# One more pair of key tiles of one query group moved from ScalarE's exponential to VectorE's, with a new written-out order

## The chip, the cores and the metric

The kernel runs on one core of a Trainium2 chip. The metric is the device time of one execution in microseconds (us); lower is better. The engines are named as in the profile: PE is TensorE, ACT is ScalarE, DVE is VectorE, POOL is GpSimd, and SP is SyncE, which only issues DMAs.

## The reference

The input `x` has 2048 rows of 640 numbers. It is normalised, goes through an attention of 32 heads of width 20 (branch A) and through a gated two-stage MLP (branch B), and the two are multiplied and added to `x`:

```python
def _A_ref(x, wqkv, wo):
    ...
    scores = jnp.einsum("bhqd,bhkd->bhqk", q, k) * (Dh ** -0.5)
    p = _softmax(scores, axis=-1)
    o = jnp.einsum("bhqk,bhkd->bhqd", p, v)
    ...
x = A_x
xn = _layernorm(x, axis=-1)
s = _A_ref(xn, A_wqkv, A_wo)
g = _silu(_B_ref(xn, B_w1, B_w2, B_w3, B_w4))
return x + s * g
```

The exponentials of the softmax are 32 x 2048 x 2048 numbers, and they are most of the work outside TensorE.

## The kernel before

**Groups.** The heads go in eight quads of four heads, the queries in four groups of 512 (`qc`). One quad and one `qc` make a group of attention work; "group 3_3" is the last query group of quad 3, and "group 4_0" comes next. There are 32 groups, the last of which (7_3) has code of its own. In a group the 2048 keys are 16 key tiles of 128.

**A key tile on ScalarE.** TensorE makes the scores of the four heads (tasks `sc...`, each one head, 128 keys by 512 queries, one PSUM bank). ScalarE takes two heads at a time through one exponential of 128x1024 (`exp_act`, L1707) into SBUF. Where one wide PSUM tile is free, one instruction takes all four heads (128x2048, L1684). One `pv` task of four matmuls (L1447) multiplies with the values and adds into the one accumulation bank of the group.

**A block on both engines.** A "block" is a pair of key tiles (`BLK`: (2,3), (6,7), (10,11), (14,15), (0,1)). `score_both` makes, for each of the two tiles, the scores of all four heads; ScalarE takes two heads of each tile, and VectorE the other two. VectorE's way to an exponential has two steps. First it turns each score tile of 128x512 into a 16-bit integer with a scale and an offset (`u...` tasks, L1729), whose bits read as bf16 are a coarse power of two. Then three shifted copies of that integer tile are made by adding a constant (`s..._1` to `s..._3`), and the four versions are multiplied with the values and added up on TensorE (`pvd...` tasks, L1629: four versions for each block, four matmuls each). A shifted copy is one VectorE instruction (L1617, 128x4096 where two blocks share one, 128x2048 where a block is alone) or one GpSimd instruction (L1615). `PP` lists which go to GpSimd: shifts 2 and 3 of the unit that starts with block 0, and shift 3 of the one that starts with block 2. A block that stands alone as number 4 (`(6, 0, 1)` in `UNITS`) has its three shifts on VectorE.

**How many blocks.** `ND[quad][qc]` says how many blocks a group has. Most groups have four; eleven of the 32 have five (1_0, 2_0, 3_0, 4_0, 4_2, 5_0, 5_2, 6_0, 6_1, 6_2, 7_0). `order` takes the key tiles that are left over for ScalarE alone.

**Two ways to make scores.** A `sc` task is one matmul that uses 32 of TensorE's rows ("row form", L1638; the four heads of a tile then run side by side), or four matmuls over all rows and 32 columns each ("column form", L1655). All other work on TensorE is in column form. In `follow` a score task next to another one gets the row form, a lone one the column form.

**What fills TensorE.** The MLP of branch B, the projections of later heads (`mm_tile`, L748) and their evictions on VectorE (`gt`, `sev`, `vev`, `bo`) stand between the score and value matmuls. In group 3_3 ScalarE also does two of the four long GELUs (L2110).

**The order.** Nothing is scheduled at run time. `program` lists some 6,950 tasks with what they read and write; `TABLE` is one long string that names the tasks in the order in which they are emitted, and after each task the PSUM banks (seven for rotating tiles, one for the accumulation) and SBUF slots that it takes. `follow` reads it, and each engine executes its tasks in the order of the string, waiting on semaphores for what a task needs. Two characters are a task, and each further one a bank or a slot.

Of the kernel before, what the change touches and what calls it, by code (L numbers as in the profile page):

```python
# [671 lines left out]
class Gen:  # L672
# [1621 lines left out]
```

## Time and profile before

| | |
|---|---|
| median of three runs | 779.2 us (778.91 to 779.86) |
| the profiled execution | 780.64 us, of which 778.9 us lie between its first and its last instruction |
| granted TensorE clock, mean | 0.997 |
| busy: PE / ACT / DVE / POOL | 767.8 / 761.1 / 701.4 / 441.3 us |
| instructions | 28,219 |

A row of a group of instructions reads: line, engine, operation, tiles, count, then busy time, the mean duration of one, and the idle time of the engine just before them with what ended it. Durations of neighbouring instructions overlap (each engine is a pipeline), so the busy time of a group, which counts overlapped time once, divided by its count is nearer to what one instruction costs than the mean duration. Matmul ends are modelled, and four matmuls of column form run side by side.

### The profile page before, as it was taken

To read this page: it belongs to the slowest core of one execution; us is meant where nothing else is said; L and a number is where in the kernel's file an instruction comes from. 1 tells how busy PE (TensorE), PEld (TensorE's weight loads), DVE (VectorE), ACT (ScalarE), POOL (GpSimd) and SP (SyncE) were. 2 spreads that over 40 slices of the span, in tenths; PEclk is the share of its full clock that TensorE was granted. 3 is DMA by queue.
4 is the path that set the end of the run, shared out by engine and by line. 5 is a ranking of instruction groups with operands and counts; after the bars stand their busy time and mean duration, and the time that the engine had idled before them with its cause. 6 is when DMAs were issued, how large, how long until landed. Compare 5 with 4: busy or idle time off the path is not lost.

```text
span 778.9 us, 28219 instructions
## 1 busy us (share of the span) xinstructions
PE 767.8 (99%) x12594; PEld 296.5 (38%) x12594; DVE 701.4 (90%) x1177; ACT 761.1 (98%) x802; POOL 441.3 (57%) x238
## 2 busy tenths in 40 slices
PE   8999999999999999999999999999999999999996
PEld 4433333334444333233534334333334333333454
DVE  8889899988999999998988889999998899997786
ACT  7999999999999999999999999999999999999995
POOL 6386745564547657566464664766553635635742
PEclk9999999999999999999999999999999999999998
DMA  5315343364112423433343232324431023114443
GB/s 173 51 57 116 97 85 77 63 163 77 20 39 46 77 64 81 81 66 75 59 115 57 24 71 56 74 58 87 111 52 33 9 54 93 21 19 109 129 142 104
DMA packets 141353, 58.13 MB, mean 75 GB/s; under 512 B 113728, under 2 KB 136432, under 8 KB 141232
## 3 DMA queue, kind: packets, MB, share of 16 engines
q1 hardware_dynamic: 141232, 56.33, 32.8%
q8 instruction: 99, 1.62, 0.9%
q14 instruction: 22, 0.18, 0.1%
HBM read 34.70 MB, written 10.33 MB: 58 GB/s over the span
## 4 chain that ended last, share of the span: by engine, by line
PE 55%; ACT 41%; DVE 2%; DMA 1%; SPq 1%; issue 0%
ACT arena L1707 36%; PE psum L748 20%; PE psum L1638 14%; PE psum L1629 9%; PE psum L1447 7%; PE psum L1655 2%; ACT arena L2110 1%; ACT arena L1684 1%; ACT arena L2018 1%; DMA arena<-in_A_wqkv_dram 1%; SPq L935 1%; PE psum L1504 1%; ACT arena L2138 1%; PE psum L1478 1%; PE psum L1508 0%; DVE arena L1729 0%
## 5 line engine op out<-in xcount | busy, mean ns | idle before, releaser
L1707 ACT ACTIVATE arena<-psum 128x1024 bf16<-128x1024 f32 x730 | 675.0, 1075 | 5.8 <-PE psum L1638 3.7
L1615 POOL TENSOR_TENSOR arena<-arena 128x2048 int32<-128x2048 int32 x92 | 330.3, 3600 | 212.9 <-DVE arena L1617 126.3
L1729 DVE TENSOR_SCALAR arena<-psum 128x512 uint16<-128x512 f32 x532 | 342.8, 682 | 30.9 <-PE psum L1638 24.4
L748 PE MATMUL psum<-arena 128*32 128x320 bf16 (+1 forms) x5808 | 335.2, 333 | 0.4 <-ACT arena L1102 0.2
L1638 PE MATMUL psum<-arena 32*128 32x512 bf16 x1872 | 242.7, 384 | 1.4 <-ACT arena L1707 0.6
L1629 PE MATMUL psum<-arena 128*22 128x512 bf16 x2128 | 186.0, 382 | 0.2
L748 PEld LDWEIGHTS psum<-arena 128*32 128x32 bf16 x5808 | 138.2, 96 | 120.8 <-issue 44.2
L1638 PEld LDWEIGHTS psum<-arena 32*128 32x128 bf16 x1872 | 65.3, 91 | 208.9 <-ACT arena L1707 111.5
L1447 PE MATMUL psum<-arena 128*22 128x512 bf16 x1452 | 138.7, 382 | 0.0
L1617 DVE TENSOR_SCALAR arena<-arena 128x4096 uint16<-128x4096 uint16 (+1 forms) x124 | 133.7, 1095 | 1.0 <-PE psum L1629 0.2
L1629 PEld LDWEIGHTS psum<-arena 128*22 128x22 bf16 x2128 | 48.0, 90 | 63.4 <-issue 42.2
L1761 POOL TENSOR_TENSOR arena<-arena 128x512 bf16<-128x512 f32 x30 | 41.5, 1383 | 32.6 <-DVE arena L1617 27.6
L1447 PEld LDWEIGHTS psum<-arena 128*22 128x22 bf16 x1452 | 35.0, 90 | 52.0 <-issue 35.1
L1655 PE MATMUL psum<-arena 128*32 128x512 bf16 x476 | 46.3, 380 | 0.3
L2103 DVE CAST arena<-psum 128x512 bf16<-128x512 f32 x48 | 32.7, 684 | 3.8 <-PE psum L748 3.6
L1314 DVE CAST arena<-psum 128x512 bf16<-128x512 f32 x40 | 27.1, 685 | 4.7 <-PE psum L748 4.3
L1926 POOL TENSOR_TENSOR arena<-arena 128x640 bf16<-128x640 bf16 x12 | 16.8, 1402 | 21.5 <-DVE arena L1860 5.5
L959 DVE BATCH_NORM_STATS2 arena<-arena 128x6 f32<-128x320 bf16 x54 | 24.4, 477 | 1.6 <-DMA arena<-in_A_x_dram 1.6
L1748 DVE STREAM_TRANSPOSE arena<-psum 128x512 f32<-128x512 f32 x30 | 21.3, 711 | 2.5 <-PE psum L1629 1.5
L1860 DVE SCALAR_TENSOR_TENSOR arena<-psum,arena 128x320 bf16<-128x320 f32 x32 | 15.5, 486 | 8.3 <-PE psum L748 8.0
L1684 ACT ACTIVATE arena<-psum 128x2048 bf16<-128x2048 f32 x12 | 22.8, 1900 | 0.0
L2132 DVE TENSOR_TENSOR arena<-psum,arena 128x320 bf16<-128x320 f32 x32 | 15.6, 489 | 7.4 <-PE psum L748 7.2
(135 smaller groups left out, 340.9 us busy)
## 6 DMA issues: line engine op xcount, KB each, us to landing
arena<-in_B_w_dram SPq DMA_DIRECT2D x48, 160.0 KB, 2.7
arena<-arena SPq DMA_DIRECT2D x124, 32.0 KB, 1.9
arena<-in_B_w_dram SPq DMA_DIRECT2D x4, 960.0 KB, 5.5
arena<-in_A_x_dram SPq DMA_DIRECT2D x8, 320.0 KB, 5.5
arena<-in_A_x_dram SPq DMA_DIRECT2D x16, 160.0 KB, 3.0
out_dram<-arena SPq DMA_DIRECT2D x16, 160.0 KB, 2.6
heads<-arena SPq DMA_DIRECT2D x120, 20.0 KB, 2.0
arena<-keys SPq DMA_DIRECT2D x28, 80.0 KB
```

Of the source, the lines that this page charges most:

```text
L748: ins = e.matmul(pb[32 * c:32 * c + 32, 0:N], lhsT(k, c), rhs(k, c), start=(k == 0), stop=(stop and k == nk - 1), tile_position=(0, 32 * c))
L1447: ins = e.matmul(pb[32 * i:32 * i + 22, 0:512], VA[:, ql, kts[i // 2], i, :], PT[:, slots[i // 2][0].slot, slots[i // 2][0].at(i % 2):slot ...
L1615: return e.tensor_tensor(dst.bitcast(I32), U[:, ub, 0:w].bitcast(I32), bass.AP(c.tensor, c.offset, [list(c.ap[0]), [0, w // 2]]), op=ALU.add)
L1617: fa if onp else lambda e, v=v, dst=dst: e.tensor_scalar(dst, U[:, ub, 0:w], EXP_B[v], None, op0=ALU.add),
L1629: ins = e.matmul(pb[32 * i:32 * i + 22, 0:512], wv, dst[:, at:at + 512].bitcast(BF16), start=first, stop=final, tile_position=(0, 32 * i))
L1638: return e.matmul(out, self.KT[32 * i:32 * i + 32, b, 128 * kt:128 * kt + 128], q, start=True, stop=True, tile_position=(32 * i, 0))
L1655: ins = e.matmul(out[32 * c:32 * c + 32, :], self.KT[:, b, 128 * kt + 32 * c:128 * kt + 32 * c + 32], self.QM[:, gb, i, :], start=True, st ...
L1684: lambda e: e.activation(self.PT[:, hp[0].slot:hp[0].slot + 2, :], self.psum[:, 512 * h0.slot:512 * h0.slot + 2048].rearrange("p (a b) -> ...
L1707: lambda e: e.activation(self.PT[:, hp.slot, :].rearrange("p (a b) -> p a b", b=512), self.banks(hs), AF.Exp, scale=cfg.scale),
L1729: T("dve", c_dve(512), lambda e, h=h, y=y: e.tensor_scalar(U[:, ub, y:y + 512], self.bank(h.slot)[:, :], a_exp, EXP_BIAS, op0=ALU.mult, op ...
L1761: return e.tensor_tensor(OnT.rearrange("p (k d a) -> p a k d", k=4, a=4), Ob[:, :].rearrange("p (a k d) -> p a k d", a=4, k=4), in1, op=AL ...
L2103: T("dve", c_dve(512), lambda e, h=h, fc=fc, i=i, G=G: e.tensor_copy(G[:, i, fc, :], self.wbank(h)[:, 0:512]), reads=[wa], writes=at, name ...
```

## The change

Group 3_3 gets a fifth block, the key tiles 0 and 1, which go through ScalarE alone before. The order and the banks of the whole program are written anew; the first 79 steps of TensorE (up to the transposes of the first tiles) and the first 23 of ScalarE stand as they were.

```diff
         self.ND[6][1] = 5
+        self.ND[3][3] = 5
...
 TABLE = (
...
-    r"`@-?{@+)?i@)#@3?|)?}(?t2s)@,2t@>%@@'@=$?~%@A#?q2u:[2v:c@C@F#@/)@.(?p@I2w@2&@&@9%@:$@G'@;$2x?o@J@?#@6(@7)@E&@5:]@B2B#2C@8(2D2E:Y2F@D%:d?s2G@H)@M@L@W)@Z#@[$@X(?r@"
...
+    r"j?f)@3?Y@*#@''@(&?l@4@+$?}$@))?|%@-?t?{?~&@,@=&@@(@>'2s&:V?q@C2t2u@A#2v2w@/%@.$@F)2x?p@2'@I@&@9'@:&@G#?o@J@;(@7)@6(@E$@?%@5@B2B&2C@8%2D2E2F@D%?r?s@H'2G@P@W&@X'@"
...
```

The two strings, read as `follow` reads them (two characters a task, then its banks), give these counts; nothing in the table is a time:

| | before | after |
|---|---|---|
| tasks | 6951 | 6959 |
| exponentials of 128x1024 in group 3_3 | 24 | 22 |
| `u` tasks of 128x512, whole program | 532 | 536 |
| shifts on DVE, two blocks wide / one block wide | 91 / 33 | 91 / 36 |
| shifts on POOL | 92 | 92 |
| `pv` tasks and `pvd` tasks in group 3_3 | 12 and 16 | 11 and 20 |
| score tasks in column form, whole program | 119 | 105 |
| runs of row-form work between column-form work | 557 | 561 |
| rounds of a run beyond its first (one 32-row strip used again in it) | 94 | 95 |
| tasks on SP / POOL | 283 / 234 | 283 / 234 |

On ScalarE 55 exponentials change places, by two places at most. On TensorE, VectorE, GpSimd and SP a good part of the tasks moves by some places. On SP, for instance, the copy of the queries for group 0_1 (`qm0_1`, L1405) now goes ahead of the two weight loads of the next heads (`ld_ws0`, L1306), with the copy `qm0_2` between them. On VectorE the four new `u` tasks stand among the evictions of the value projection (`vev1`); the first new shift stands ahead of the first `u` of group 4_0, the second and the third behind five and seven of them.

More of the change, by code (lines that the diff above doesn't have):

```diff
@@ new lines @@
+    r"W&X&g#7&o$c%B$<%t)&Y%u%v&a$?%w%m(G%o&w$$E&x$>&y&z$d&{$F*?$*<'&h%E*@#*;($G%x&|*A'&6(&7$='($')$f$e'*%D$I'+*=%',*9#$g*8$'-$h&8*:&&9&:$H&}$*5'*4($i%y$j**#*+$*6#&~&;"
+    r"'#'$'%$k*>*,$%Z('&%P#%Q%U%%[%R%]%V%W%F$%G%H%I%^%X%z%S%K'%L%J%M%N%T%Y%{&%|%}%_%~(H*C(*B'%O*2%*1&&#(I*3)&&'&'&$&(';$&)&%&**-&*.%&+'<*D('=&H&'>&-'?&.&I*/%&2%'@&J&K"
+    r"&L&,*0&3&M*`&*_'*K(*J)*I%*H$&<*a&&?&*N(K(L'A&@&0&A*M&B*L%&4%&C*Q)+(&+''&5&D*P%*O$*7+)$*T*E'/%'0&=&*F*S)'1*X'*W&&>'2*G&q$*Y#&r'3'4*R%*Z#*[$&s*U&t*]'&u+3(*h&+2'&v"
@@ new lines @@
+    r"*V*i%*k+4(*c#*b$'I$*l'J'K*d%'L'M+$(+%''N*^+T&i+&)*o&*m$*p#*n%&p'5$*r'6'7*q''8+5'+6(*s'9*e+7#*f&':*g%+D#+C$+**v'B$'C*j&'D'U#'d'E'F'V&N'W'G'X+E$'Y+=&+<%&E'Z+.)+/("
+    r"*y+#+>)+8'O&'P'Q'R+0%'S'](+:&'T+9'+;(+X$+['^+W#++(+,)*x+Z'_'`+-&'a+K&+J'+`$'b+_#'[+?+L#+b'H+o%+H(+G)'.*{+c''+1+I'*|&F&+r+U'+V&*w&G+Y)&O',*(+n%,+)*u&P-.*z,,(+u#,"
+    r"-&,.'+q+M*t,/%+x+v$+^(+])'f(+y'g+a'*}+@&+A',J$+|,K#'e*~+B#'h(Q'i'j+i(&/+h),L&'k+F'l#'m+N+j#'n,;#+e%,:$+f&+d'o,>,&+g$+t(+s),='p,0+w),B#'q,8&,9%,A$+k,E,D,<%+l'+m("
@@ new lines @@
+    r"'r$'s+p('t+O,G%,?#,@$,H&'u'c'v,I'(J'x#'y'w'z'{,C#+P'|,N%,O&,W)'},X(,M,P$,),[,w$'~,x#+},Z,y(,Q',R(,_&,`%,#,',c(M$,S&,q$,p#,b,F+z,t',r'(N(#-?%,s(->&(O,T+{,e,d,(-1"
+    r"#,~),u)-2$-@&-#(,4'+~-4,%-$%,v,5&-5(%&,$(&,6',f,^(,1$,]),2%('(R(P((,3)(),i(+#(,(Y(-,a#,z%-8&,{$,7(*,l(v,h,|$(.-;(a-%)-&(-9#(/-<-'),g,U%-H$,V&(0,}.`,k,Y'-K-G)-/("
+    r"-0'-(-J-3$-N#-L$-M%-O&,o#8+Q-Q,j-P)(1$-j'-R-k(,m(o(2-l'-U-7#-6$-F&-E%(3,n-:%-A(-B'($-)(4-X(5-I#(7&-*-=(6(8(9-g%-C$.%&-h$-p)(:-s-_-i%(;.$'(Z%(<([.&)(]-w%(=+R0605"
@@ new lines @@
+    r"-c#-x)-d$-[(^-{-e(-D-v&-u'+S-z(_-m-y#(`.2).1%-}$-~#-V.4-W.#%-q&.)(.('.5-Y-Z.*&.'-t-`$-a#(S$&1-b).+&.9%.8(.,'(T.<(U.-$-T-n#.;/8%-o$(V-r'-f.?/9&-S(W/:)...6((X.0$."
+    r"7'./#-^-|.:&(>(}(w((@(x(y.@.3(.I&(z({.J#.B-]&b.H(?&&Z.E(A(|.>.M%.L$(B.=.N%.d'(C.c#.S(.T)0I)(E.g0J.U&.K.O$.P%.f.k'0K.Q#.n.V(.W).j#.C3$-+.m0L/k'.i$.h%.R/n.G.X$.l'"
+    r"0M-,.y).b'.a(.z#0N.Y.e#.F.}.q$.p%.s&.A.|.r%.D.t'07&.Z/%)08.u$/#%/(.~$/$(.o/'09/&(.x&.w'/F).v--/I0:.{&0;/?%/@$/6(/5)0</)/A'0=#.[/4/+0>0?/7&/U$/V#/<&/=%0@(F/.0A/>"
@@ new lines @@
+    r"$0C$0B0D0E0F/W%0G/J(/K'/{&/|%/*0H0P/N(/;/B0O/-(~$(D/}&/,/S(/R')#/1.])$/T$/d#/E$/C&/D%)%/H/0/G#(h)&/Z(/g/Y'/X/[)45/~$)'/M&/j#0#%///P(b$0$$(c/](/m/^'/L&(d/c%/_%/O"
+    r"/f/a#/b$(e(f)D/e'0%0)((g/h&0*'/i%/`)K/l&/t/Q0R$0S0T0U/q0&$0V0+$0'(/30X#/20W4O(0Y/w0Z4R0[0]49)48(4E#4F$0^0-%0,&/s4G#0r4;/o0(/r4<4H'0.%4I(4@$4N#/z4C/p4J(/u.^4Q4>&"
+    r"4=%4U$/v0Q4A&4X4V#4S)4T(4?'/x4B0/4W)4k$4L&4M%/y4Y0_#4P%0`46(47)4j#0a004]4K4l$4:#0b0e)._0f0c4`0d4q$5##4r%0g5&0h4s(0i5((4w)5)'0j4f5*'4D4z4u$4v%4x#(p)(q)(4{4y%4~'5"
@@ new lines @@
+    r"+(5,)(r5%(s5-&4c56$57%01(t4_52#(u5/'51)50(4b5:#555.)=53)4a5I$5J%540k58#59&4^5K&5s5<4}(4n'4|)4Z5;4o&5$'4d5B5H)>&)?4p#5T)4g%5S(4h$)@5?4e5U))A5')B5>4i%4[)C5E5b)5a&"
+    r"5L(5M'4t5d5e5N'5X#5W$))()*5[#)+5Q(5Y&5Z'5P)),5^4m5R(5`$5_#5])-).5=5c$025D5u(5t'5v)5w&5y5O)R5x%6K%5z6L$5~#5@5F5V6M')/6%6*(5}'6+)5G6$6,)5A7H5|#6'&6(%5k5C5f6)&61)5"
+    r"i6I'6H(6J(5{$5m5g5l(i(5j6460&5h036#$(j63(k6/(6.'5n67)68&6^$6_#62#(l6:6&(m6;6-6b%65)66(6O'(n6N6P&69))E&0l)6)F0n)G)H6>6Q')I046n%6m$6S)6R(6G6T&6=)J0m)0o6A6?5o6o$6Y"
@@ new lines @@
+    r"#0p6X'6g)6f(6<6[6@6h#6U)o6V&6]6W%)L#)M6Z&6j)6`#6i(6a$)N6c)O6k')P6D6{&6d6|%6e7#()Q6B6w#6t(6u)6v$6z6l6x)7<'7=&6y)0()17>#)26q)6~#6p(6}$)37$716r%7:&79')47%6C7;)6s)5"
+    r"72#75(76)73$6F7(77()7()87?)974$):7+7@&);7A%6E)S&)<)T7.)U7Q$)a)V7P%)Y)W787T)7J')X)v7K&7L)7I(7&7O7'7M'7g$7R#Ef7h%7-7N7)7k$8))7U8((7S'5p7,7B7V8*#7b#7c$7a%7`&7*7e70"
+    r"7d&7/8>)7f8?()Z&7C7j'8@(7i$8,&8-%)[7m7W)]80%7l8%)8&(8/')^7D8''7v827y8<&8.$8;%)_818=&86'84(83)7n)`)b'87)8+898E%8F&)}5q8~)h85#)c885r)d8G$8K)8e(8d'8N8:)e8f#)f8h%8g"
@@ new lines @@
+    r"&)g8L#8C)8A8i%8O8B()i#)j0q7p8D')k8n%8o&8l$8k#)l)m8m&)p%7s8j)n)q)r8p#8u#8R)8S'8V8v$8w))s)t7q8I&)u8J%8H8M(8U8P$8r'8Q#8s(8q)w$8t%)x7r)y)z8Y8T&){)|7{(7]&7z'7[%7x7|'"
+    r"7o7t7u7w)~$8]7^#*#*$*%*&*(9-'9B&9%%9&(8`Et&90Eu8xEv*'8ZEw9)Ex3#En'Eo9(EyEpEqEh%EiEj8^9EEr7EEk9,%Es9C)9;'9<#Ez)E{E|9?3%0s:}7FE}9FEl*)E~0u'0vF#11&0w8cEg0xEm8a1213"
+    r"0y9/14151%)34%16351&360z371'7Y%9>8[1(7X$1)7G383H#1*3I7Z(3J3K393L3&)3;&3M3'3(3)3*8b93'7}(3+7~)3<9I8_:o3=8#)3>92&F$3?3B(3C3@9L94%3D3E3F96)9$$9##3G8X9'&F%9S&9T%9@'"
@@ new lines @@
+    r"9A(8W0t7_9D$0{&0|9U#0}8$3-'3.0~3/95(8y1#1=#3:301>97)9+%1$9O9*&1?1@9.(319:(?C99)9d#32988z1A9='9g9J9r%9e$9q&911B9s%17&9h9l)9t(9u'18:W9R9v(198{9W%9o9V&9k$1:1;9n9G9"
+    r"X'9b(9c':&)1<9w8|9f):)1U'9H9Z&9[%:%#1V:(9Y9]$Lt1W9|(9{):-':^9K9}#:01X:*%:+&:,#9Q:/1Y:.'9_'1C$9^(1Z1D9M1E:39`(9x$9j&9i%9y#8}9P9z&:X1F1G:91+#1,1H1-1.1/9m%9a:#(:b1"
+    r"0:$)9N1b&:'(1c:>':_:Z:@$:A%?M&1d:`1e?P:B$9p1f:=(:?%1I$1g1J:<1K:K$1L1M:L(1N:1:C:G':H(2Z$2[:62]9~2^:I%2_?G#:D&:E%?F$2`:M:T:7?I:F$?D(?^'?E)::?J:8?H#?N$?V%?W&?a?d#:"
@@ new lines @@
+    r"'@T:eA,AX$:QA5#A8(A6$@OA+A7)@t@{A>'@uA9)A'&A&%:U@QAA@U@wA*'BZ2g&2h2i2j@vA:%2kA=%@yAC'A<$A?&@x:fA@(2l@z:i:mAD(1[$@|1]1^:R1_AG&1`ABAa$Ab#AE%A4A;:k1h#Ac#1aAH1iAY)A"
+    r"F&AZ(1jAI1kA['1l1t&1u1v1m1wAO1xAf%Ae$Ah&Ag)1yA_'A^(AUAi%@}Ak2$&2%2&2'Aj2(A`)Ax&Aw%An$AJ2)A]Ay&Aq20$Am(Ao#Al'21Ar2223Ap(AR24Au%B(&At$25AdB+2m&A{)Av'B)'A|(AsB,2n2"
+    r"oA}$2p2qA~%B#&B0'2rB$(B/$B2AzAQB-)B.(2<&B32=B1#2>2?ALB'$B&%BD'BC&2@B*&AP2a%2bB%2A2c2dBE'B92e2y$BQ%BG$BH#2zBI$2{2|2f2}@~BR&AN;mAMBS(2~BA'CP#CQ$B@(B?;s2H$BB%B62I2"
@@ L2262, in bass_recurrent_scan__mha_block__mixer_s_mlp__prompt_kernel @@
+    r"o#onp5of#nuoy$npnvnwoz)omp$#nxp+o$p<'p%(o{$p=ovopoqotosp@#p>p&owo%pAoxp?o|'o}p6p7p8p:p9p;pD$pBpH#pEpIpCpFpJpGpKpLpM")
 def bass_recurrent_scan__mha_block__mixer_s_mlp__prompt_kernel(nc, A_x, A_wqkv, A_wo, B_x, B_w1, B_w2, B_w3, B_w4, out):
```

179 lines of the change are left out of this document (74 added, 105 removed).

## The prediction

> **What bounds the kernel now.** I read the page's busy times first, then the chain of work that ended last, then stretches of single groups, then prices of single instructions. The busy times:
>
> ```profile
> span 778.9 us, 28219 instructions
> PE 767.8 (99%) x12594; PEld 296.5 (38%) x12594; DVE 701.4 (90%) x1177; ACT 761.1 (98%) x802; POOL 441.3 (57%) x238
> PE 55%; ACT 41%; DVE 2%; DMA 1%; SPq 1%; issue 0%
> L1707 ACT ACTIVATE arena<-psum 128x1024 bf16<-128x1024 f32 x730 | 675.0, 1075 | 5.8 <-PE psum L1638 3.7
> L1729 DVE TENSOR_SCALAR arena<-psum 128x512 uint16<-128x512 f32 x532 | 342.8, 682 | 30.9 <-PE psum L1638 24.4
> L1638 PE MATMUL psum<-arena 32*128 32x512 bf16 x1872 | 242.7, 384 | 1.4 <-ACT arena L1707 0.6
> ```
>
> PE and ACT are both full, and the chain changes between them. ACT stood idle only 5.8 us before its 730 exponentials. DVE has about a tenth of the span free, POOL almost half. The chain in order of time shows long runs on ACT, and, between them, stretches where it lies on PE. Group 3_3 lies in one of these (from its first exponential at 367.5 us to the next group's at 402.9):
>
> ```profile
> 144.02 14.80 ACT arena L1707 x16
> 245.37 49.62 ACT arena L1707 x54
> 621.39 62.47 ACT arena L1707 x68
> by line: PE psum L748 49.4%; PE psum L1638 17.0%; PE psum L1629 14.3%; PE psum L1655 9.1%; PE psum L1447 8.5%; DVE arena L1314 2.0%; issue 0.2%
> ```
>
> The last row is the chain asked for 367.5 to 403 us alone: no ACT in it. So ACT's exponentials are the pace of most of the kernel, but in this group the page puts PE first. How full each engine is, group by group (the columns are length, then busy time and count for PE, PEld, DVE, ACT, POOL, then clock, DMA share, GB/s; the stretches are 3_1, 3_3, 4_0, 4_1 and 4_2):
>
> ```profile
> 315.40:343.80 28.40, 28.08 (x393) 8.71 (x385) 27.93 (x47) 28.40 (x32) 14.99 (x9) 1.00 0.41 74
> 367.50:402.90 35.40, 35.25 (x627) 15.46 (x619) 31.93 (x54) 35.35 (x30) 15.76 (x11) 1.00 0.37 77
> 402.90:423.00 20.10, 20.10 (x343) 8.00 (x339) 16.55 (x27) 20.10 (x23) 13.68 (x8) 1.00 0.43 87
> 423.00:444.10 21.10, 21.10 (x361) 7.91 (x357) 18.73 (x31) 21.10 (x25) 11.68 (x5) 1.00 0.16 23
> 444.10:463.30 19.20, 19.20 (x338) 7.98 (x334) 15.66 (x25) 19.20 (x23) 12.01 (x4) 1.00 0.40 73
> ```
>
> The last two rows are the nearest thing that the trace has to this change. Group 4_1 has four blocks, group 4_2 five, so two exponentials fewer (25 and 23 instructions touch the two stretches). Both are full on PE and ACT alike, and the chain is on PE in both. The group with five blocks is 21.10 - 19.20 = 1.90 us shorter.
>
> **The change part by part.**
>
> ScalarE loses two exponentials of 128x1024 in group 3_3. Instructions overlap, so the price is the pace: 14.80 / 16 = 0.925, 49.62 / 54 = 0.919, 62.47 / 68 = 0.919 us. Two are 1.84 us, and the pair of groups above says 1.90. ACT's queue holds nothing new.
>
> TensorE's prices stand in pieces of the chain of group 3_3:
>
> ```profile
> 367.91 0.33 PE psum L1638 x4
> 368.23 0.33 PE psum L1629 x4
> 369.64 0.22 PE psum L1629 x4
> 374.05 0.22 PE psum L1655 x4
> ```
>
> Four matmuls of a value step cost 0.22 us (third row), and 0.33 where row-form scores come next (second row): the change of form costs 0.11. Four scores in row form cost 0.33 (first row). So a run of row-form scores costs 0.33 + 0.11 = 0.44 us, for one to four heads; one lone score in column form costs 0.22 (fourth row). The fifth block brings four `pvd` tasks and takes one `pv` away: 3 x 0.22 = +0.66. From the counts of the two orders: 14 scores fewer in column form, -14 x 0.22 = -3.08; four runs more, +4 x 0.44 = +1.76; one more round inside a run, +0.22. Sum: -0.44 us of 778.9, over the whole program. TensorE's work does not grow, and falls by a quarter of ScalarE's saving.
>
> VectorE gains four `u` and three shifts of one block's width:
>
> ```profile
> L1617 DVE TENSOR_SCALAR arena<-arena 128x4096 uint16<-128x4096 uint16 x91 | 111.7, 1243 | 0.8
> L1617 DVE TENSOR_SCALAR arena<-arena 128x2048 uint16<-128x2048 uint16 x33 | 22.2, 686 | 0.2 <-PE psum L1629 0.2
> POOL arena L1615 <- DVE arena L1617: 126.3, 28, 14.0
> DVE arena L1729 <- PE psum L1638: 1.3, 3, 0.8
> ```
>
> Busy time by count: 4 x 342.8/532 + 3 x 22.2/33 = 2.58 + 2.02 = +4.6 us. In 367.5 to 402.9 DVE is busy for 31.93 of 35.40, so 3.47 us are free there, and in the next stretch 20.10 - 16.55 = 3.55 more. With a saving of 1.84 the two stretches are 53.66 long and hold 31.93 + 16.55 + 4.60 = 53.08 us of DVE work: it fits by 0.6 us over both, and not in group 3_3 alone. What hides it is that much of DVE's work there is eviction for later use (the projections of the next heads), and that two of the three shifts stand behind `u` tasks of 4_0. If that cover fails, ACT waits for it (the second rival). I put it at nothing for the sum. That DVE can run this full without harm is in the row of 3_1: 27.93 of 28.40 us, with ACT at 28.40.
>
> GpSimd gets no instruction. Its shifts often wait for DVE's (126.3 us in 28 waits, third row above), but it is busy for only 15.76 of the 35.40 us here, so a delay by three shifts of 0.67 us, 2.0 us, has cover. The Trainium skill, "SBUF — State Buffer", section "SBUF: two separate sides", says that VectorE's two-port modes and GpSimd share a port pair that the one who starts first holds for its whole instruction. By it each new shift could be held up by one GpSimd shift; that is the third rival.
>
> SP's queue gets nothing new, but steps move past one another. The one with a visible price is at the start: the weight loads for the next heads now stand behind the copies for groups 0_1 and 0_2 (last row: from issue to landing, of L1306).
>
> ```profile
> 29.64 5.49 SPq L1306 DMA_DIRECT2D arena<-in_A_wqkv_dram  x2
> 40.31 13.44 SPq L1405 DMA_DIRECT2D arena<-arena  x8
> DMA to landing us min/median/max: 2.5/2.9/5.7
> ```
>
> The eight issues of the copies end at 53.75 us, and the second load goes behind them, about 19 us later than now. Its user, the query projection of those heads, comes behind the key projection's 80 matmuls in TensorE's order; I take zero, and at most the median landing of 2.9 us if it is needed at once.
>
> The rest of the new order has no row: a move may add or remove a wait. Bounds: of ACT's idle time only 5.8 us stand before exponentials in all, so nothing better than -1 us can come from it; and a group's waits differ from its neighbour's by some tenths (35.40 - 35.35 in 3_3, none in 4_1 and 4_2), so some three of the 32 groups falling out by 0.3 give +1 us. I take zero.
>
> Sum: -1.84 us on ScalarE, which TensorE follows because its own work falls too. The profiled execution was 780.64 us (778.9 in its span, 1.7 around it), 1.44 above the median of the runs. The change is a difference, so it goes onto the median: 779.2 - 1.84 = 777.4 us.
>
> **The rivals.**
>
> *TensorE keeps the pace; the gain is its own 0.44 us to about 1 us.* For it: the chain of group 3_3 is PE alone, and so it is in the groups behind it, before it turns to ACT (the chain asked for 403 to 490 us, and for 549 to 610 us):
>
> ```profile
> by line: PE psum L748 33.7%; PE psum L1638 28.5%; PE psum L1629 20.5%; PE psum L1447 13.8%; PE psum L1655 3.7%; PE psum L1286 0.2%
> by line: ACT arena L1707 75.3%; ACT arena L2110 17.3%; ACT arena L1684 2.9%; ACT L2110 2.1%; ACT L1707 2.1%; ACT arena L2138 1.9%; issue 0.1%
> ```
>
> PE cannot start later work sooner than its own queue allows. Counting TensorE's work along the two orders at the prices above, what stands ahead of the scores of group 5_0 falls by some 1.5 us, but most of it comes back by group 6_1 (0.4 left). Against it: PE's waits are themselves mostly for ACT:
>
> ```profile
> PEld psum L1638 <- ACT arena L1707: 111.5, 296, 0.6
> ```
>
> and they can shrink when ACT is earlier. Time: 779.2 - 0.44 to 779.2 - 1.0, say 778.4. The Trainium skill, "Perfetto Trace Analysis", section "Identifying the Most-Contended Engine", would settle this for ScalarE: it takes occupancy for Scalar and Vector and calls busy time of matmuls a bad measure for Tensor. By it ACT at 98% is the one to relieve and the whole 1.84 us come through; the chain's 55% for PE speak the other way, and I give neither the whole.
>
> *VectorE becomes the bound behind the GELUs of group 3_3, and the kernel is slower.* Place: 367.5 to 402.9 us. If all 4.6 us have to be done there, DVE needs 31.93 + 4.60 = 36.53 us, and with the 0.47 us that it stood idle in its fullest stretch (28.40 - 27.93) 37.0 us: 1.6 more than the group's length now. The late `u` hold PSUM banks, PE's next scores wait for these, and ACT for the scores. It decides from the point where DVE's work in the group passes 35.4 us, that is if less than 1.1 us of it slides into 4_0. Time: 779.2 + 1.6 = 780.8, and more if evictions wait in turn. For it: DVE is the engine with the added work. Against it: its free 3.55 us in the next stretch, and that DVE waits for PE in the group now (1.3 us, above).
>
> *The shared port.* Each of the three new shifts waits for a whole GpSimd shift, 3.60 us as a mean:
>
> ```profile
> L1615 POOL TENSOR_TENSOR arena<-arena 128x2048 int32<-128x2048 int32 x92 | 330.3, 3600 | 212.9 <-DVE arena L1617 126.3
> ```
>
> At half an instruction each that is 5.4 us on DVE; less the 3.5 us that are free in 4_0, +1.9: 781.1 us. Against it: the 91 wide shifts have a mean of 1.243 us, near 111.7 / 91 = 1.23 by busy time, so long holds must be rare, and GpSimd is idle for over half of this stretch.
>
> **How the numbers follow.** About 0.2%, 1.56 us, is what a measurement of this kernel can tell from no change. The forecast, 777.4, is 0.23% down and lies just beyond it: 0.42. TensorE's pace, within the bound: 0.34. VectorE late, 780.8 and more, just beyond the other side: 0.18. The port: 0.06. So faster 0.42, same 0.34, slower 0.24. Low end: the saving and the 1 us of waits, 776.4. High end: VectorE late and 1 us of waits from new places, 781.8. About 0.06 lie below and 0.1 above.
>
> **What would show it.** Right if L1707 has 728 instructions, its busy time near 673.2, with ACT's idle time still near 5.8 us before them; L1729 536, L1617 127, L1629 2144, L1447 1448, L1655 420. The stretch of group 3_3 is then near 33.6 us with DVE over 33. TensorE's pace shows as more idle time on ACT before L1707, released by PE L1638, from group 4_0 on. VectorE late shows as PEld L1638 waiting for DVE L1729 and a group 3_3 of 36 us or more. The forecast is wrong if group 3_3 does shrink and the end does not come earlier, or if ACT's idle time rises by over 1 us.

## The result and the profile after

The changed kernel takes 778.11 us (median of 18 runs, 777.25 to 779.17) against 779.77 us of the kernel before (18 runs beside it, 778.91 to 780.56): ratio 0.9980, 95% interval 0.9974 to 0.9987. The gain is 1.66 us, by the interval 1.0 to 2.0. The interval leaves no change out, but the gain lies only just beyond the 0.2%, 1.56 us, that the prediction took as the least that can be told. The forecast was a difference of 1.84 us, to 777.4; 0.6 of the 0.7 us between 777.4 and 778.11 are there because the three runs of before that it stood on had a median of 779.2.

The page of the kernel after, its busy times, its chain and the groups that answer to those of before (line numbers are one higher):

```profile
span 776.4 us, 28161 instructions
PE 765.6 (99%) x12564; PEld 295.5 (38%) x12564; DVE 705.4 (91%) x1184; ACT 759.4 (98%) x800; POOL 439.6 (57%) x238
PE 49%; ACT 46%; DVE 4%; DMA 1%; SPq 0%; issue 0%
L1708 ACT ACTIVATE arena<-psum 128x1024 bf16<-128x1024 f32 x728 | 673.4, 1079 | 6.1 <-PE psum L1639 4.2 <-PE psum L1505 1.1
L1730 DVE TENSOR_SCALAR arena<-psum 128x512 uint16<-128x512 f32 x536 | 345.1, 682 | 27.7 <-PE psum L1639 21.3
L1639 PE MATMUL psum<-arena 32*128 32x512 bf16 x1886 | 244.0, 384 | 2.0 <-ACT arena L1708 1.0
```

All counts are those that the prediction gave. ScalarE's idle time before exponentials went from 5.8 to 6.1 us, VectorE's busy time from 701.4 to 705.4. The chain has moved towards ScalarE (41% to 46%).

Where the time came from shows best on ScalarE's own timeline around the first GELU of group 3_3. The columns are start, length, instruction and count, and in brackets the idle time before it. ACT_TABLE_LOAD is ScalarE's change from the exponential to the GELU. First before, then after:

```profile
360.12 15.00 ACT L1707 ACTIVATE arena<-psum 128x1024 bf16<-128x1024 f32 x16
375.13 1.28 ACT L2110 ACT_TABLE_LOAD   x1
376.43 10.54 ACT L2110 ACTIVATE arena<-arena 128x6144 bf16<-128x6144 bf16 x2
```

```profile
360.15 11.18 ACT L1708 ACTIVATE arena<-psum 128x1024 bf16<-128x1024 f32 x12
371.67 1.94 ACT L1708 ACTIVATE arena<-psum 128x1024 bf16<-128x1024 f32 x2 [0.33 <-PE psum L1639]
373.63 1.28 ACT L2111 ACT_TABLE_LOAD   x1
374.92 10.54 ACT L2111 ACTIVATE arena<-arena 128x6144 bf16<-128x6144 bf16 x2
```

Sixteen exponentials became fourteen, and the GELU begins 1.51 us earlier. The starts of the groups up to 3_2 differ by 0.3 us at most where both orders begin a group alike, and group 3_3 starts at 367.50 and 367.41. The starts of single exponentials, laid side by side, say how the 1.51 is made up. (An exponential is named by its quad, query group, key tile and pair of heads: 3_3_7_1 is the second pair of key tile 7 in group 3_3.) At 3_3_7_1 the changed kernel is 1.90 us ahead (0.09 of it had been there at the group's start), at 3_3_4_0 it is 1.75, at 3_3_2_0 1.35. So the full price of two exponentials, 1.81, arrives, and then two waits for TensorE's scores take 0.15 and 0.41. The last exponential ahead of the GELU, which starts soon after a wait, then lasts 1.02 us instead of 1.18, and since the GELU waits for its end, 0.16 come back: 1.51 at the GELU. Behind the GELUs 0.07 are lost, and at the first exponential of 4_0 it is 1.44. So group 3_3 is 1.34 us shorter (1.81 - 0.15 - 0.41 + 0.16 - 0.07). At the starts of the later groups the changed kernel is ahead by 1.42 to 1.63 us, and at VectorE's last work by 1.56. One group made nearly the whole gain.

Could the new order alone have made it, with no exponential taken away? In the kernel before, ScalarE's exponentials in group 3_3 start 0.904 us apart wherever nothing holds them, and all waits beyond that add up to 0.24 us. An order with the same 24 exponentials in this group could have saved no more than that.

The stretches 3_3, 4_0 and 4_1 of the kernel after (columns as in the prediction):

```profile
367.40:401.40 34.00, 34.00 (x608) 14.91 (x604) 32.81 (x54) 33.62 (x27) 18.21 (x18) 1.00 0.21 50
401.40:421.50 20.10, 19.98 (x328) 7.67 (x332) 17.84 (x28) 20.10 (x23) 11.75 (x4) 1.00 0.30 76
421.50:442.50 21.00, 21.00 (x347) 8.03 (x343) 19.10 (x31) 21.00 (x24) 10.64 (x4) 1.00 0.28 55
```

VectorE is busy for 32.81 of 34.00 us in 3_3, and 1.3 us more than before in 4_0 (17.84 against 16.55), which keeps its length of 20.1.

### The profile page after: what moved, and what is told of

It reads as the page before. It is cut to its first block, busy times and chain, and to the rows that moved or that the text cites. A ratio compares the mean times of both kernels' runs of the same rounds, so it can differ in the third digit from the quotient of the medians.

```text
span 776.4 us, 28161 instructions
## 1 busy us (share of the span) xinstructions
PE 765.6 (99%) x12564; PEld 295.5 (38%) x12564; DVE 705.4 (91%) x1184; ACT 759.4 (98%) x800; POOL 439.6 (57%) x238
## 4 chain that ended last, share of the span: by engine, by line
PE 49%; ACT 46%; DVE 4%; DMA 1%; SPq 0%; issue 0%
ACT arena L1708 40%; PE psum L749 19%; PE psum L1639 12%; PE psum L1630 8%; PE psum L1448 6%; DVE arena L1730 1%; ACT arena L1685 1%; ACT arena L2111 1%; PE psum L1656 1%; ACT arena L2019 1%; ACT arena L2139 1%; DVE arena L1618 1%; DMA arena<-in_A_x_dram 1%; PE psum L1505 1%; PE psum L1479 1%; PE psum L1509 0%
## 5 line engine op out<-in xcount | busy, mean ns | idle before, releaser
L1616 POOL TENSOR_TENSOR arena<-arena 128x2048 int32<-128x2048 int32 x92 | 330.2, 3598 | 214.8 <-DVE arena L1618 126.1
L749 PE MATMUL psum<-arena 128*32 128x320 bf16 (+1 forms) x5808 | 339.5, 333 | 0.4 <-DVE arena L2104 0.2
L1656 PE MATMUL psum<-arena 128*32 128x512 bf16 x420 | 40.9, 380 | 0.0
L2111 ACT ACTIVATE arena<-arena 128x6144 bf16<-128x6144 bf16 x4 | 21.1, 5316 | 0.0
```

Source lines behind the costliest of these rows:

```text
L749: ins = e.matmul(pb[32 * c:32 * c + 32, 0:N], lhsT(k, c), rhs(k, c), start=(k == 0), stop=(stop and k == nk - 1), tile_position=(0, 32 * c))
L1616: return e.tensor_tensor(dst.bitcast(I32), U[:, ub, 0:w].bitcast(I32), bass.AP(c.tensor, c.offset, [list(c.ap[0]), [0, w // 2]]), op=ALU.add)
L1656: ins = e.matmul(out[32 * c:32 * c + 32, :], self.KT[:, b, 128 * kt + 32 * c:128 * kt + 32 * c + 32], self.QM[:, gb, i, :], start=True, st ...
```

## The experiments

A median of some eleven runs (nine and six for two of the kernels) has an interval of about 0.8 us either way, too wide for single terms of this sum. The length of group 3_3 in the profiled execution, from its first exponential to that of 4_0, is much finer: 35.36 us before, 34.02 after. How finely such a length repeats shows behind it: from the first exponential of 4_0 to that of 7_2 all eight kernels with the new order took 317.43 to 317.44 us. I read the length of the group beside the ratio. All ratios are to the kernel before, as it ran beside each series (medians 780.2 to 780.5).

| kernel | median us | ratio, 95% interval | group 3_3, us | its own baseline |
|---|---|---|---|---|
| changed kernel | 778.11 | 0.9980, 0.9974 to 0.9987 | 34.02 | 35.36 |
| two exponentials short, old order | 779.74 | 0.9994, 0.9985 to 1.0003 | 35.15 | 35.36 |
| TensorE short, old order | 780.33 | 0.9999, 0.9990 to 1.0008 | 35.36 | 35.36 |
| both short, old order, first (clock at half in part of the group) | 779.50 | 0.9986, 0.9977 to 0.9995 | 36.30 | 35.36 |
| both short, old order, again | 779.45 | 0.9994, 0.9983 to 1.0004 | 34.97 | 35.36 |
| two short behind the GELUs, old order | 779.97 | 0.9996, 0.9984 to 1.0007 | 35.33 | 35.36 |
| extra exponentials, new order | 778.91 | 0.9982, 0.9974 to 0.9991 | 34.22 | 34.02 |
| value tasks short, new order | 778.27 | 0.9976, 0.9967 to 0.9984 | 34.02 | 34.02 |
| VectorE short, new order | 778.19 | 0.9976, 0.9966 to 0.9986 | 34.01 | 34.02 |
| three value tasks ahead, new order | 779.09 | 0.9987, 0.9978 to 0.9995 | 34.63 | 34.02 |
| one value task behind, new order | 778.18 | 0.9971, 0.9959 to 0.9982 | 34.12 | 34.02 |
| two more short, new order | 778.44 | 0.9979, 0.9970 to 0.9987 | 34.02 | 34.02 |
| TensorE short, new order | 778.23 | 0.9980, 0.9971 to 0.9989 | 33.90 | 34.02 |

**ScalarE relieved alone, in the old order.** The edit, in the exponential:

```
- e.activation(PT[slot], banks(hs), AF.Exp)
+ e.activation(PT[slot][:, :, 0:n], banks(hs, n), AF.Exp)   # n = 32 for 3_3_1_0 and 3_3_0_1, else 512
```

> The kernel before in its own order; of the two exponentials that the change takes away (3_3_1_0 and 3_3_0_1) only 32 of 512 columns in each bank are computed, so ScalarE is relieved by about 2 x 0.7 = 1.4 to 1.5 us and nothing else changes (TensorE's and VectorE's instructions and their order stay). The forecast's theory (ScalarE sets the pace into group 3_3, TensorE follows): 1.2 to 1.5 us off, ratio 0.9981 to 0.9985, made before the first GELU of group 3_3 and kept to the end. TensorE's theory (the gain of the change is its own 0.44 us and its new order): 0 to 0.3 us off, ratio 0.9996 to 1.000, with ScalarE idle for TensorE's scores instead.

Measured: group 3_3 shorter by 0.21 us, ratio 0.9994. On ScalarE's timeline of this kernel the time that the short exponentials save comes back as idle time, and TensorE works without a gap meanwhile:

```profile
367.71 1.14 ACT L1707 ACTIVATE arena<-psum 128x1024 bf16<-128x1024 f32 x2 [0.37 <-PE psum L1638]
369.66 4.69 ACT L1707 ACTIVATE arena<-psum 128x1024 bf16<-128x1024 f32 x5 [0.81 <-PE psum L1638]
```

A miss for the forecast's theory as I had put it: 1.4 us less on ScalarE alone, at the same place, bring 0.2.

**ScalarE loaded again, in the new order.** A second, tiny exponential goes ahead of each of eight:

```
+ e.activation(spare[:, k], banks(hs, 4), AF.Exp)
  e.activation(PT[slot], banks(hs), AF.Exp)
```

> The changed kernel with its order; ScalarE gets eight very short extra exponentials (4 columns in each of two banks, into a spare buffer that nobody reads), one each ahead of the last two exponentials of group 3_2 and the first six of 3_3, all before the first GELU; at an estimated 0.2 us each they put some 1.6 us back onto ScalarE, and on no other engine. The forecast's theory: 1.2 to 1.6 us are given back (less what falls into ScalarE's two waits of 0.5 us there), ratio to the kernel before 0.9995 to 1.000. TensorE's theory: the changed kernel stays where it is, ratio 0.998. VectorE's theory (its added work takes part of the gain): also ratio 0.998, since VectorE gets more time.

The price in that text was wrong. The first tiny exponential and the full one behind it:

```profile
365.71 0.33 ACT L1705 ACTIVATE arena<-psum 128x8 bf16<-128x8 f32 x1
365.77 1.19 ACT L1706 ACTIVATE arena<-psum 128x1024 bf16<-128x1024 f32 x1
```

The next instruction starts 0.06 us later, so eight of them put not 1.6 but 0.4 to 0.5 us onto ScalarE. The GELU came 0.28 us later for it (group 3_3, counted from its first tiny exponential, is 0.20 longer, the rest is in the last two exponentials of 3_2), the other part fell into the two waits. Too small a dose for the ratio (0.9982), but in the trace ScalarE's added time does come through, as the forecast's theory has it, less what the waits absorb.

**The value tasks and VectorE's work of the fifth block.**

```
- matmul(pb, wv, dst[:, at:at + 512])
+ matmul(pb, wv, dst[:, at:at + cols])   # cols = 64 for the four pvd3_3_4_*
```

> The changed kernel; the four value tasks that the fifth block brings (4 matmuls each, into rows of all four heads) have 64 columns instead of 512, so part of the sum over that block is left out; TensorE is relieved by about 4 x 0.19 = 0.76 us in group 3_3, behind the GELUs. The forecast's theory: no change against the changed kernel, ratio to the kernel before 0.9975 to 0.9985. TensorE's theory: 0.76 us more, ratio 0.997.

```
- tensor_scalar(U[:, y:y + 512], bank, ...)
+ tensor_scalar(U[:, y:y + cols], bank[:, 0:cols], ...)   # cols = 64 for the four new u; the shifts 256 instead of 2048
```

> The changed kernel; the work that the change brings to VectorE is cut: the four new u tasks have 64 columns instead of 512 (about -1.6 us) and the shifts of the fifth block 256 columns instead of 2048 (about -1.6 us), so most of that block's exponentials are left out. The forecast's theory (all of this is hidden): no change against the changed kernel, ratio to the kernel before 0.9975 to 0.9985. The theory that VectorE's time or its port with GpSimd takes part of the gain (the 0.2 us by which the result stays behind the forecast): 0.2 to 1 us more, ratio 0.9965 to 0.9975.

Stretch 3_3 in the one, then in the other:

```profile
367.10:401.10 34.00, 33.70 (x608) 15.14 (x605) 32.71 (x54) 33.62 (x27) 18.24 (x18) 1.00 0.20 49
367.60:401.60 34.00, 34.00 (x612) 14.89 (x608) 30.51 (x54) 33.63 (x27) 18.20 (x18) 1.00 0.23 54
```

TensorE's busy time falls by 0.3, VectorE's by 2.3, and the length of the group doesn't move by more than 0.01. What the fifth block brings to TensorE and VectorE behind the GELUs is hidden, and the theory that VectorE or the port takes part of the gain falls. The ratios (0.9976 both) overlap with the changed kernel's.

**TensorE alone, and both, in the old order.** After these four I held that TensorE and ScalarE are both full ahead of the GELU, so that only both cuts together would gain. The edit cuts nine of TensorE's tasks there:

```
+ cols = 64   # pvd3_2_2_2, 2_3, 0_1, 3_1 and the five steps of w3_1_9, instead of 512
```

> The kernel before, its order and all its exponentials; TensorE alone is relieved ahead of the first GELU of group 3_3: four value tasks of group 3_2 (pvd3_2_2_2, 2_3, 0_1, 3_1) and the five steps of the filler tile w3_1_9 have 64 columns instead of 512 (the rest of these columns is left out), 9 x 0.19 = 1.7 us less for TensorE. New theory, formed after the first four runs (both engines are full ahead of that GELU, so either alone gains nothing and only both together do): group 3_3 from its first exponential to the next group's stays at 35.2 to 35.4 us, 0 to 0.2 us off. A pure TensorE theory: 1.2 to 1.7 us off, group 3_3 at 34 us. The forecast's theory (ScalarE alone sets the pace): 0, as the new one.

> The kernel before and its order with both cuts at once: the two exponentials 3_3_1_0 and 3_3_0_1 with 32 of 512 columns per bank (ScalarE 1.4 us less) and TensorE's nine tasks with 64 columns (1.7 us less). New theory (both full): 1.2 to 1.4 us off, group 3_3 at 34.0 to 34.2 us, ratio to the kernel before 0.998, though ScalarE's cut alone gave 0.2 us in that group. The forecast's theory: the same as ScalarE's cut alone, 0.2 us. A pure TensorE theory: the same as TensorE's cut alone.

TensorE's cut alone: 35.36 us, no change to 0.01; TensorE doesn't set the pace there by itself. Both cuts: the first profiled execution can't be read, because TensorE's clock was 0.57 just there (third column from the right):

```profile
370.00:374.00 4.00, 4.00 (x37) 0.82 (x33) 3.12 (x5) 2.86 (x4) 0.00 (x0) 0.57 0.26 33
```

So it was run again.

> The run with both cuts once more (the kernel before; exponentials 3_3_1_0 and 3_3_0_1 cut to 32 columns per bank, nine tasks of TensorE to 64 columns), because the profiled execution of the first had TensorE's granted clock at 0.50 in 370 to 372 us, just ahead of the GELU in question. New theory (both engines are full ahead of that GELU): with the clock at 1.00 there, group 3_3 at 34.0 to 34.2 us, 1.2 to 1.4 us off. The forecast's theory: as ScalarE's cut alone, 35.2 us.

With the clock at 1.00: 34.97 us, 0.39 less than before (the intervals of the two ratios overlap). That is a miss for my new theory, which wanted 34.0 to 34.2. The trace says what stood in the way. Two matmul rows of TensorE and ScalarE's exponential around 367.8 us in this kernel:

```profile
367.24 0.24 PE L1631 MATMUL psum<-arena 128*22 128x64 bf16 x8
367.84 0.39 PE L1640 MATMUL psum<-arena 32*128 32x512 bf16 x4 [0.36 <-ACT arena L1709]
368.27 1.02 ACT L1709 ACTIVATE arena<-psum 128x1024 bf16<-128x1024 f32 x1 [0.37 <-PE psum L1640]
```

TensorE has finished early and waits 0.36 us for ScalarE; then ScalarE waits 0.37 for TensorE. The scores of 3_3_0_0 go into banks 3 and 4, which the exponential 3_2_1_0, two places ahead, has to have read. Only when that full exponential ends, at 367.79, can the scores be made, and 0.48 us behind its end the next exponential starts. The short exponential between them lasts only 0.40 us in the trace and cannot fill the 0.9 us that a full one would have taken. A shortened exponential is not a removed one: it keeps its place in the rotation of the bank pairs.

ScalarE's second wait, 0.62 us ahead of 3_3_3_1, has another cause. Ahead of the scores of 3_3_3_1 TensorE's queue has the value task pvd3_2_3_1, and this waits for one of VectorE's shifts (TensorE's waits in 366 to 375 us):

```profile
PE psum L1631 <- DVE arena L1618: 0.8, 1, 0.8
```

With ScalarE's cut alone the same wait was 0.81 us, with TensorE's queue full. So right behind TensorE's queue stand the banks and VectorE's shift, and relieving the queue gains only what lies between them. The cut on TensorE alone ran into the same two: it waited 0.36 us for ScalarE and 0.75 for VectorE.

**The same cut behind the GELUs.** The same edit as the first, for 3_3_9_1 and 3_3_13_0.

> The kernel before and its order; of two exponentials of group 3_3 that stand behind its GELUs (3_3_9_1 and 3_3_13_0) only 32 of 512 columns per bank are computed; ScalarE 1.4 us less, the same cut as in the first run of this series, 27 us later. If the GELUs are what made that first cut worth only 0.2 us (they come 6 us behind it, and TensorE, whose order is fixed, has too few waits in these 6 us to follow), then here TensorE can follow over the next groups, by its own waits of about 0.6 us in each: 0.2 to 0.5 us off by the start of 4_0, and 1.0 to 1.4 us by 5_0, kept to the end. If TensorE is as full as ScalarE everywhere: 0 to 0.3 us off at the end here too. The forecast's theory: 1.4 us off at once.

Group 3_3 is shorter by 0.04 us, and the start of 5_0 and that of 7_2 come 0.08 earlier: the GELUs are not what made the first cut worth little. This is what the expectation gives for a TensorE that is as full as ScalarE there too. ScalarE has two waits again, of 0.39 and 0.89 us:

```profile
395.48 0.22 ACT L1707 ACTIVATE arena<-psum 128x64 bf16<-128x64 f32 x1 [0.39 <-PE psum L1638]
396.60 3.77 ACT L1707 ACTIVATE arena<-psum 128x1024 bf16<-128x1024 f32 x4 [0.89 <-PE psum L1638]
```

**The order of the changed kernel, partly undone.** Only rows of the order table move: pvd3_2_2_3, 2_2 and 3_1 go ahead of the scores of 3_3_7_1. In the changed kernel they stand behind those of 3_3_2_0, pvd3_2_2_3 between the two score tasks of 3_3_6_0 and the other two behind them. Two scores that stood alone between them (3_3_6_0y and 3_3_15_0y) fall into row form by the move.

```
  pvd3_2_3_3
+ pvd3_2_2_3, pvd3_2_2_2, pvd3_2_3_1
  sc3_3_15_0
```

> The changed kernel with one part of its order undone: three value tasks of group 3_2 (pvd3_2_2_3, 2_2 and 3_1, 3 x 0.22 = 0.66 us of TensorE) stand ahead of the scores of 3_3_7_1 again, as in the kernel before, instead of behind those of 3_3_6_0; nothing else differs. New theory: TensorE's scores for the last exponentials ahead of the GELU come 0.4 to 0.66 us later, and so do the GELU and everything behind: group 3_3 at 34.4 to 34.7 us. The forecast's theory (ScalarE's two exponentials fewer are the gain, the order is immaterial): no change, 34.0 us.

```profile
360.23 9.35 ACT L1708 ACTIVATE arena<-psum 128x1024 bf16<-128x1024 f32 x10
369.89 2.07 ACT L1708 ACTIVATE arena<-psum 128x1024 bf16<-128x1024 f32 x2 [0.31 <-PE psum L1639]
372.36 1.94 ACT L1708 ACTIVATE arena<-psum 128x1024 bf16<-128x1024 f32 x2 [0.39 <-PE psum L1639]
```

ScalarE now waits ahead of 3_3_7_1 too, the GELU comes 0.60 us later, the group is 0.61 us longer, and this stays to the end; the ratio goes from 0.9980 to 0.9987. Expected were 0.4 to 0.66. The order is not immaterial: 0.66 us of TensorE's work, put in front of the scores again, take back almost half of the group's gain.

**The waits that are left.** One more value task moved behind, in the changed kernel:

```
- pvd3_2_2_1   (ahead of sc3_3_2_1y)
...
  sc3_3_6_0
  pvd3_2_2_3
+ pvd3_2_2_1
  sc3_3_6_0y
```

> The changed kernel with one value task more (pvd3_2_2_1, 0.22 us of TensorE, and 0.11 for a change of form) moved from ahead of the scores of 3_3_2_0 to behind those of 3_3_6_0, where ScalarE waits for TensorE in the changed kernel. New theory: the exponential 3_3_2_0 and the GELU start 0.15 to 0.3 us earlier, group 3_3 at 33.7 to 33.85 us, ratio to the kernel before some 0.0003 lower. The forecast's theory: no change, 34.0 us.

> The changed kernel with two more exponentials ahead of the GELU cut short (3_3_0_0 and 3_3_3_1, 32 of 512 columns per bank; ScalarE 1.4 us less, the rest of these two left out). New theory: TensorE's scores set the last exponentials ahead of the GELU there, so 0 to 0.1 us off, group 3_3 at 33.9 to 34.0 us. The forecast's theory (ScalarE's pace): 1.4 us off, 32.6 us.

> The changed kernel with TensorE cut where ScalarE waits for it: the five steps of the filler tile w3_1_10 and the value task pvd3_2_2_1 have 64 columns instead of 512 (6 x 0.19 = 1.1 us less; the rest of these columns is left out). New theory: ScalarE's two waits of 0.15 and 0.47 us ahead of the GELU go, the GELU starts 0.5 to 0.6 us earlier, group 3_3 at 33.4 to 33.5 us, which is the forecast's 33.6; and ScalarE's pace stops it there. The forecast's theory: nothing, 34.0 us. A pure TensorE theory: 1.1 us, 32.9 us.

The one task moved: 3_3_2_0 starts 0.22 us earlier, as expected, but 3_3_6_0 not at all, and the group ends 0.10 later. The edit does not do what the expectation says: the exponential 3_3_6_0 needs both its score tasks, and the value task still stands ahead of the second, 3_3_6_0y. So what moving it behind both would bring stays untried. (The ratio, 0.9971, is the lowest, but its interval holds 0.9980, and the trace gives no gain to put it down to.) Two more exponentials cut short: 34.02, nothing, with 1.27 us of idle time behind them (first line below). TensorE cut by 1.1 us: 33.90, where 33.4 was expected; ScalarE then works almost without a break up to the table load (second line; 0.12 us of idle time ahead of 3_3_6_0 are too short to show in it). But 3_3_2_0 starts 0.63 us earlier and 3_3_6_0 only 0.22: it starts 1.33 us behind 3_3_2_0 instead of 0.92, because TensorE waits for ScalarE in turn (third line, TensorE's weight loads in 369 to 372 us):

```profile
369.42 2.14 ACT L1708 ACTIVATE arena<-psum 128x1024 bf16<-128x1024 f32 x2 [1.27 <-PE psum L1639]
360.44 12.34 ACT L1710 ACTIVATE arena<-psum 128x1024 bf16<-128x1024 f32 x13
PEld psum L1641 <- ACT arena L1710: 0.8, 1, 0.8
```

The scores of 3_3_6_0 stand in one run with those of 3_3_0_1 and 3_3_7_0, which need the banks of 3_3_4_0. Helped at 3_3_2_0, ScalarE loses most of it again one exponential later. No version here is shown to beat the changed kernel.

## Why the prediction was right, step by step

*ScalarE, -1.84.* Right in size: 1.81 us arrive by 3_3_7_1. That ScalarE loses the two whole exponentials is the source of the gain: the old queue held only 0.24 us of waits in this group, and the extra exponentials show ScalarE's time coming through. But not all of it comes through. The sign that I gave, a group of 33.6 us, was missed: it is 34.02, and 0.4 us are lost in waits. That the medians (1.66) lie so near 1.84 is in part luck, since their interval is wider than this loss.

*"TensorE follows because its own work falls too."* Right in outcome, wrong in reason. The 0.44 us were counted over the whole program, and the gain was made in some 6 us of one group, ahead of its GELUs; cutting the block's value tasks behind them changed nothing. What counts is what stands ahead of the scores there. Taking two exponentials out of the order takes their score runs and their places in the bank rotation with them, and the new order also puts value tasks behind: from the scores of 3_2_1_0 to the last ones of 3_3_6_0 TensorE's queue takes 7.23 us before (366.11 to 373.34) and 6.29 after (365.67 to 371.96). With the three value tasks back in front, 0.73 of 1.34 us remain. What would remain if only the two exponentials went, and the rest of the old order stayed, no run shows: the short exponentials (0.21 of 1.4 us, and 0.00 with two more cut in the new order) kept their scores and their banks, and so say too little. I read from the order, and did not try, why the old one had the three value tasks in front: with two exponentials more there, the seven SBUF slots for exponentials are full, and 3_3_6_0 has to wait for a value step of group 3_3, which comes behind all of 3_2's.

*"The rest of the new order: zero."* This is the term that was mis-sized: the trace gives 0.15 + 0.41 of new waits, inside the bound of +1. ScalarE's idle time of the old kernel bounds what an order can save, but in a kernel where both queues are kept full it says little of what one can cost: three rows of the order are worth 0.61.

*VectorE, +4.6 us at nothing.* Right: busy time +4.0 on the page, 1.3 more of it in 4_0, just above the 1.1 at which the rival was to decide, and a cut of 2.3 us in 3_3 moves nothing. VectorE in the group stayed at 32.81 where I had written over 33. That the long GELUs, in which it works on without ScalarE, give it the room is my reading and was not tried. *GpSimd and SP at nothing.* Right: GpSimd's waits for VectorE's shifts are 126.1 us in all (126.3 before), and group 0_1, the first behind the moved loads, starts 0.12 us earlier than before, not later.

*The rivals.* TensorE's pace was near the truth in kind and wrong in place: ScalarE's idle time did grow by waits for its scores, though in 3_3 and not from 4_0 on, and it cost 0.56 instead of 0.8 to 1.4. VectorE late and the port did not happen. The profile's chain, all TensorE in this group, and its occupancy, 98% for ScalarE, were both true: the two are coupled through the banks, and in these tests either one's cut alone gave 0.00 to 0.21.

## What to carry to other kernels

Where two engines are both full and hand each other buffers in a fixed order, price a change by what it takes out of every queue in that stretch, and not by one engine's busy time. Once the first of them was relieved here, the banks or a third engine stopped the gain within some tenths of a microsecond. Shortening an instruction is a poor test of removing it: it keeps its buffers and its place. When run times differ by less than their interval, the length of one stage in the trace, which repeated here to 0.01 us, still tells parts apart; only the clock of that stage has to be looked at first.

## What the runs showed of the hardware

An exponential of 128x1024 lasts 1.02 us by itself but starts 0.905 us behind the one before when its scores are there; one of 128x8 lasts 0.18 us alone (0.33 to 0.45 in a row) and costs the next only 0.06. The Trainium skill, "Perfetto Trace Analysis", section "Optimizing Scalar/DVE Operations", gives about 51 ns for what a ScalarE instruction on PSUM occupies beside its data, and warns that the latency shown is about twice that. The 0.06 us are near the first figure; the length shown is three times the price here, not twice (0.18 against 0.06). My 0.2 us in the expectation was the shown length taken for the price.

TensorE's clock fell to half for about 3.4 us (370.0 to 373.5 us) in one of the two profiled executions of the kernel with both cuts, right after a stretch in which TensorE was busy for 1.25 of 2 us; the other execution had the same stretch at 1.00. That group took 36.30 us in the one and 34.97 in the other. And the last part of the program, from the first exponential of 7_2 to the start of VectorE's last work, took 54.8 to 56.2 us in executions of kernels that are alike there, and group 3_3 began at 366.8 to 367.7 us, while the 317.4 us between 4_0 and 7_2 repeated to 0.01 in the new order: most of the spread of the run times comes from places that the change doesn't touch.
